# Keeping the issue order of all engines through the last gate units, and five smaller edits

## The chip, the cores and the metric

One core of a Trainium2 chip runs the whole program. The metric is the device time of one execution in microseconds, of which the median of several runs is taken. All arithmetic is float32; TensorE works on pairs of rounded parts (a high part and the low rest, both of type fp32r), three products for one.

## The reference

Three layers follow one another over 4 sequences of 768 tokens. The first is a delta-rule attention with a state of 48 x 48 per head, the second a gated layer that mixes tokens with a 768 x 768 matrix, the third a channel mix with a shift by one token.

```python
for t in range(S):                                     # attention, 4 x 8 heads
    y[t] = q[t] @ state
    state += beta[t] * outer(k_n[t], v[t] - k_n[t] @ state)
h = gelu(x @ w_in); u, v = split(h)                    # gated layer, tanh form of gelu
v_n = (v - mean(v)) / sqrt(var(v) + 1e-6) * g_ln
x = x + (u * (w_sg @ v_n + b_sg)) @ w_out
xk, xr = mix(mu_k, x, x_prev), mix(mu_r, x, x_prev)    # channel mix
out = sigmoid(xr @ w_r) * (relu(xk @ w_k) ** 2 @ w_v)
```

## The kernel before

**Stages.** The attention runs in chunks of 64 tokens, two chunks to a group, six groups (`g`). `run` (L829) issues one stage of each of two streams of chunks, then counts the step `point[0]` up by two in `tick`, and then fills PE's time with `fill` (L680) from the list of gate units. A gate unit is a block of `x @ w_in`: a `v` unit (L611) gives 128 tokens of one sequence, 9 matmuls of 512 columns and then a gelu on ACT (L625); a `u` unit (L662) gives two sequences, 18 matmuls of 256 columns, a gelu (L672) into `ug`, and a store to `u_d`. The attention's result of a group is stored to `xT` (`store_x`, L560); some steps later, by `LAGX` or for the last group `LAGE`, `x_split` (L581) rounds it into `xh` and `xl`, and two steps on the group's units are in the list.

**Rows' scaling.** Each `v` goes through `ln_steps` (L631): bn_stats and bn_aggr on DVE, then for two sequences at once a negated mean and a power of -0.5 on GpSimd (L645 to L648, the exponent is the tile `nhalf`), then `apply` (L651) on ACT (L652) `yield`ed some steps later. The result goes to `vn_d` in DRAM, or, for sequence 0 of the last two groups, straight into a ring block by `to_ring` (L844).

**Weights.** `narrow` (L147) turns a piece of a weight, which comes as 64-bit words, into a high and a low part: load on SP, conversion L157 on ACT, L162, L164, L166, L168 on DVE, an integer add L170 on GpSimd, then `split` (L110) with L113 for the high part on ACT and L116 for the low part on GpSimd. `resident` uses it for `w_in`, `scratch` for the other weights (8 pieces of `w_out` and 12 of `w_k` from the pool `stg`; `w_r` and `w_v` from another pool), which go back to DRAM. A part of the pieces of `scratch` is issued during the attention, the rest by `side` (L968), which `mix` and `project` call.

**Between attention and mixing.** After the attention's scope the kernel opens 8 PSUM banks (`ps`) and the pools `wq2` and `vr` on the memory that the attention's pools `ap1` and `ap2` leave. It loads `b_sb` and the first three blocks of `ws1` (the second half of `w_sg`; `fetch_ws1`, L935, through `staged`, L233), begins the first mixing with 60 matmuls on 4 banks (`begin`, L924), and then loops (L947) until the last gate units are through: `background`, `fill(5)`, and one `split_ws1` (L938) a turn, which rounds a block on ACT and DVE and loads the block three further on. Then `wo` is reloaded on GpSimd's queue, and the mixing runs over 4 sequences x 2 halves of the tokens: `mix` (L994) with 18 matmuls, `w` on DVE (L1004, L1006), `gh` on ACT and `gl` on DVE, and `project` (L1011). From then on comes the channel mix.

**What sets the order.** A planner orders each engine's instructions by modelled times and priorities in program order; a load or an operation further down may go ahead of one that it takes to be not ready. In a `manual_schedule` scope the engines named issue their own instructions of that scope in program order; instructions from outside the scope may still be placed between. SP, which issues most transfers, is in no scope. Before, PE, ACT, DVE and GpSimd are in one during the attention (L244), and PE alone (L892) from there to the end.

Of the kernel before, what the change touches and what calls it, by code (L numbers as in the profile page):

```python
# [7 lines left out]
F32 = mybir.dt.float32  # L8
# [8 lines left out]
B, H, S, D = 4, 8, 768, 48  # L17
DM = 384
FF = 1024
HF = 512  # L20
P = 128
# [25 lines left out]
NT_ = (3, 3, 3)  # L47
LNW = 1
LAGX = 6
LAGE = (4, 1)  # L50
LASTP = 134
FROM = 124
LAGU = 2
# [13 lines left out]
def vw(t, off, dims):  # L67

    a = t[:]
    return bass.AP(a.tensor, a.offset + off, [list(a.ap[0])] + [list(d) for d in dims])  # L70
# [9 lines left out]
def fused_kernel(  # L80
# [17 lines left out]
    nc = tc.nc  # L98
    V, A, G, T = nc.vector, nc.scalar, nc.gpsimd, nc.tensor

    cp = ctx.enter_context(tc.tile_pool(name="cp", bufs=1))
    dp = ctx.enter_context(tc.tile_pool(name="dp", bufs=1, space=bass.MemoryType.DRAM))
    stg = ctx.enter_context(tc.tile_pool(name="stg", bufs=2))
# [6 lines left out]
    def split(eng_hi, eng_lo, src, hi, lo):  # L110

        if eng_hi is A:
            A.activation(hi, src, AF.Copy)  # L113
        else:
            eng_hi.tensor_scalar(hi, src, 1.0, None, op0=ALU.mult)
        eng_lo.tensor_tensor(lo, src, hi.bitcast(F32), op=ALU.subtract)  # L116
# [30 lines left out]
    def narrow(dram, i, j, hi, lo, cw=CW, pool=stg, lag=JLAG, parts=None):  # L147

        w = CW if pool is stg else cw
        raw = pool.tile([P, 2 * w], U32, name="raw", bufs=NRAW if pool is stg else 2)
        nc.sync.dma_start(out=raw[:, :2 * cw], in_=dram[i * P:(i + 1) * P, j:j + cw].bitcast(U32))
        w_lo = vw(raw, 0, [(2, cw)])
        w_hi = vw(raw, 1, [(2, cw)])
        yield 0
        yield 0, lambda: A.activation(w_lo.bitcast(I32), w_lo, AF.Copy, scale=2.0 ** -29)  # L157
        a = pool.tile([P, w], U32, name="na", bufs=NNA if pool is stg else 2)[:, :cw]
        af = a.bitcast(F32)
        t1 = cw / 1920 + 0.16  # L160
        t2 = cw / 960 + 0.16
        V.tensor_scalar(a, w_hi, 0x7FFFFFFF, None, op0=ALU.bitwise_and)  # L162
        yield t1
        V.tensor_scalar(af, af, E_LO_F, E_HI_F, op0=ALU.max, op1=ALU.min)  # L164
        yield t1
        V.tensor_scalar(a, a, 3, 0x3FFFFFFF, op0=ALU.logical_shift_left, op1=ALU.bitwise_and)  # L166
        yield t1
        V.scalar_tensor_tensor(a, w_hi, 0xC0000000, a, op0=ALU.bitwise_and, op1=ALU.bitwise_or)  # L168
        yield t2
        G.tensor_tensor(a.bitcast(I32), a.bitcast(I32), w_lo.bitcast(I32), op=ALU.add)  # L170
        if hi is None:
            hi, lo = (raw[:, e * cw:e * cw + cw].bitcast(F32R) for e in range(2))
            parts.append(raw[:, :2 * cw].bitcast(F32).rearrange("p (x n) -> p x n", x=2))
        yield lag, lambda: split(A, G, af, hi, lo)

    def resident(dram, pool, name, nblk, n, j0=0, j1=None):


        j1 = j1 or n
        hi = pool.tile([P, nblk, j1 - j0], F32R, name=name + "_hi", bufs=1)  # L180
        lo = pool.tile([P, nblk, j1 - j0], F32R, name=name + "_lo", bufs=1)
        return hi, lo, [lambda i=i, j=j: narrow(dram, i, j, hi[:, i, j - j0:j - j0 + CW],
                                                lo[:, i, j - j0:j - j0 + CW], lag=0)
                        for i in range(nblk) for j in range(j0, j1, CW)]
# [16 lines left out]
    def reload(dh, dl, pool, name, nblk, n, tag):  # L201
        parts = []
        for d, x in ((dh, "_hi"), (dl, "_lo")):
            t = pool.tile([P, nblk, n], F32R, name=name + x, tag=tag + x)
            G.dma_start(out=t, in_=d.rearrange("c p n -> p c n"))
            parts.append(t)
        return parts
# [20 lines left out]
    def turn(tiles, shape, dtype=F32):  # L228
        tiles.append(tiles.pop(0))
        pool, tag = tiles[-1]  # L230
        return pool.tile(shape, dtype, name=tag, tag=tag, bufs=1)

    def staged(src, n):  # L233
        x = turn(sts, [P, HF])[:, 0:n]
        nc.sync.dma_start(out=x, in_=src)
        return x

    with ExitStack() as at:
        ap1 = at.enter_context(tc.tile_pool(name="ap1", bufs=1, side="right"))
        ap2 = at.enter_context(tc.tile_pool(name="ap2", bufs=2, side="right"))  # L240
        ps1 = at.enter_context(tc.tile_pool(name="ps1", bufs=1, space=PSUM))
        ps2 = at.enter_context(tc.tile_pool(name="ps2", bufs=2, space=PSUM))
        ET = mybir.EngineType
        at.enter_context(tc.manual_schedule(  # L244
            engines={ET.PE, ET.Activation, ET.DVE, ET.Pool}))

        wv_hi, wv_lo, in_jobs = resident(w_in, fp, "wiv", 3, FF, HF, FF)
        wu_hi, wu_lo, j1 = resident(w_in, fp, "wiu", 3, FF, 0, HF)
        in_jobs += j1
# [57 lines left out]
                    if i == 0:  # L307
                        E.memset(SQ[o][0][h][r:r + 64, :, 0:D], 0.0)
        G.memset(xT[:, :, :, 0:1], 0.0)
        nhalf = ap1.tile([P, B], F32, name="nhalf")  # L310
        G.memset(nhalf, -0.5)

        def gram(g, parts=((0, 64),)):
# [224 lines left out]
        def st_y(s, o):  # L538
# [13 lines left out]
            if s % 2:  # L552
                store_x(g, o, ysts[o])
                after(LAGX if g < NG - 1 else LAGE[o], lambda: splits.append((g, o)))
            if o == 1:
# [20 lines left out]
        later, vstat, streams, point = [], {}, [], [0, 0]  # L576

        def after(n, f):
            later.append((point[0] + n, f))
# [51 lines left out]
        def ln_steps(g, b, v):  # L631
            mv, vs = vstat[g]
            n = 2
            st6 = fp.tile([P, 6], F32, name="st6")
            V.bn_stats(out=st6, in_=v)
            yield 0.6
            V.bn_aggr(out=mv[:, b], in_=st6)
            yield 0.1
            if b % n == n - 1:
                b0 = b + 1 - n  # L640
                var = fp.tile([P, n], F32, name=f"var{n}")
                yield 1, None
                rs = fp.tile([P, n], F32, name=f"rs{n}")
                nm = fp.tile([P, n], F32, name=f"nm{n}")
                G.tensor_scalar(var, mv[:, b0:b + 1, 1], EPS, None, op0=ALU.add)  # L645
                G.tensor_scalar(nm, mv[:, b0:b + 1, 0], -1.0, None, op0=ALU.mult)
                G.tensor_tensor(rs, var, nhalf[:, :n], op=ALU.pow)
                G.tensor_tensor(nm, nm, rs, op=ALU.mult)  # L648
                yield 2, None

                def apply(i):  # L651
                    A.activation(vs[b0 + i], vs[b0 + i], AF.Identity, bias=nm[:, i:i + 1],  # L652
                                 scale=rs[:, i:i + 1])
                    if b0 + i == 0 and g >= NG - 2:
                        to_ring(0, g, vs[0])
                    else:
                        after(1, lambda: nc.sync.dma_start(out=vn_d[b0 + i, g], in_=vs[b0 + i]))

                for i in range(n):
                    yield LNW, lambda i=i: apply(i)  # L660
# [19 lines left out]
        def fill(n):  # L680
            n += owed[0]
            while n > 0 and (units or opened[0]):
                if not opened[0]:
                    done = min([i for i, _ in running] + [n_jobs - len(jobs)])
                    ready = [u for u in units if done >= (6, 12)[u[2]]]
                    if ready:
                        units.remove(ready[0])
                        opened[0] = ready[0][1]()
                    else:
                        break  # L690
                w, f = opened[0].pop(0)
                f()
                n -= w
            owed[0] = min(n, 0)
            if n > 0 and point[0] < 144:
                idle[0] += n
                keep_warm(int(idle[0]))
                idle[0] -= int(idle[0])
# [3 lines left out]
        def keep_warm(n):  # L702

            if n > 0:
                o = bank()[:].rearrange("p a b -> p (a b)")
                for _ in range(n):
                    T.matmul(o, lhsT=warm, rhs=vw(warm, 0, [(0, 4), (1, P)]), start=True, stop=True)
# [136 lines left out]
        def to_ring(b, c, vst):  # L844
            t = turn(rb, [P, 2 * HF], F32R)
            vh, vl = ring[b, c] = (t[:, 0:HF], t[:, HF:2 * HF])
            split(A, G if c % 3 and (b or c > 4) else V, vst, vh, vl)

        def fetch_pair(t, i):
            src = w_sg[2 * i * P:2 * (i + 1) * P, 0:DM].rearrange("(c p) t -> p c t", p=P)  # L850
# [37 lines left out]
            fill(1)  # L888


    pe = ctx.enter_context(ExitStack())
    pe.enter_context(tc.manual_schedule(engines={mybir.EngineType.PE}))  # L892
    ps = ctx.enter_context(tc.tile_pool(name="ps", bufs=8, space=PSUM, reuse_waits="tile"))
    wq2 = ctx.enter_context(tc.tile_pool(name="wq2", bufs=1, side="right", reuse_waits="tile"))
    vx = ExitStack()
# [37 lines left out]
    ahead, got = [], []  # L933
# [13 lines left out]
    while later or splits or units or streams or opened[0]:  # L947
        background(2)
        units.sort(key=lambda u: (u[0][0], u[2]))
        fill(5)  # L950
        point[0] += 1
        if ahead:
            ahead.pop(0)()
    for f in ahead:
        f()
    fl.close()
    wo = reload(wo_dh, wo_dl, wq2, "wo", 4, DM, "w2")

    mx = ExitStack()
# [213 lines left out]
```

## Time and profile before

| | us |
|---|---|
| median of 3 runs | 802.19 |
| lowest and highest | 800.7, 803.46 |
| profiled execution, its time | 803.6 |
| its span | 801.9 |
| PE busy | 721.8 (90%) |
| DVE, ACT, GpSimd busy | 524.5, 359.6, 202.7 |

The span is what the profile covers, from the first to the last instruction. L12 is line 12 of the kernel. PE is TensorE's matmuls, PEld its weight loads, POOL is GpSimd, SP the engine that issues transfers, SPq its queue. The granted clock is a share of TensorE's full clock. A wait is idle time of an engine just before an instruction, put down to the work that ended last before it could start.

### The profile page before, as it was taken

What the parts mean: (1) busy time and instruction counts of PE and PEld (TensorE: products, weight loads), DVE (VectorE), ACT (ScalarE), POOL (GpSimd) and SP (SyncE); (2) the same over time, 40 slices, a digit from 0 to 9 for tenths busy, and PEclk for the clock granted to TensorE, in tenths of its full rate; (3) what the DMA queues carried; (4) which work ended last, traced back from release to release, by engine and by line L of the source; (5) the groups of instructions that cost most, each with busy time, mean ns of one, the idle gap of its engine ahead of it and who ended that gap; (6) DMA issues with size and microseconds to landing.
All of it is one profiled execution on the core that took longest, in us unless ns stands there. A gap on an engine that the chain in (4) does not pass through costs nothing.

```text
span 801.9 us, 23562 instructions
## 1 busy us (share of the span) xinstructions
PE 721.8 (90%) x10126; PEld 655.9 (82%) x10126; DVE 524.5 (65%) x1090; ACT 359.6 (45%) x732; POOL 202.7 (25%) x247
## 2 busy tenths in 40 slices
PE   3478998898989988879869999999999999999998
PEld 3335677777877877769769898899999999999998
DVE  6989679699697896643447684658755555554441
ACT  2225455555655656652523223216644544543330
POOL 3254333344432434442414254211000000000000
PEclk9979999999999989998989989999999999999999
DMA  8323354364463636635596546146200000000000
GB/s 236 81 67 89 95 128 111 105 167 150 114 170 113 170 100 171 187 106 165 173 297 197 180 143 228 62 156 161 67 20 30 11 21 31 11 20 30 11 21 29
DMA packets 82152, 88.66 MB, mean 111 GB/s; under 512 B 24704, under 2 KB 65024, under 8 KB 82048
## 3 DMA queue, kind: packets, MB, share of 16 engines
q1 hardware_dynamic: 76816, 77.92, 32.4%
q0 software_dynamic: 4800, 9.04, 4.1%
q8 instruction: 79, 1.29, 0.7%
q10 hardware_dynamic: 432, 0.20, 0.1%
q14 instruction: 25, 0.20, 0.1%
HBM read 56.60 MB, written 25.82 MB: 103 GB/s over the span
## 4 chain that ended last, share of the span: by engine, by line
PE 52%; DVE 19%; DMA 10%; issue 4%; ACT 4%; POOL 3%; SPq 1%; ACTq 0%; DVEq 0%; POOLq 0%
PE ms L144 33%; PE ms L919 4%; DVE sg L348 3%; PE ms L668 3%; PE rk L456 2%; PE ms L616 2%; DMA raw<-in_w_v_dram 2%; POOL na L170 2%; DMA st<-in_w_sg_dram 2%; PE ms L544 1%; PE sps L530 1%; DVE r L448 1%; PE rk L510 1%; DMA raw<-in_w_r_dram 1%; DVE sg L386 1%
## 5 line engine op out<-in xcount | busy, mean ns | idle before, releaser
L144 PE MATMUL ms<-wvh,sh 128*128 128x384 f32 x192 | 64.9, 338 | 0.0
L144 PE MATMUL ms<-wvl,sh 128*128 128x384 f32 x192 | 64.9, 338 | 0.0
L144 PE MATMUL ms<-wvh,sl 128*128 128x384 f32 x192 | 64.8, 338 | 0.0
L144 PE MATMUL ms<-xm_hi,sw0h 128*128 128x384 f32 x192 | 64.1, 334 | 0.0
L144 PE MATMUL ms<-xm_lo,sw0h 128*128 128x384 f32 x192 | 64.1, 334 | 0.0
L144 PE MATMUL ms<-xm_hi,sw0l 128*128 128x384 f32 x192 | 64.1, 334 | 0.0
L170 POOL TENSOR_TENSOR na<-na,raw 128x256 int32<-128x256 int32 (+2 forms) x43 | 37.1, 863 | 106.7 <-DVE na L168 86.8
L919 PE MATMUL ms<-ws1h,g 128*128 128x384 f32 x192 | 51.1, 340 | 5.8 <-ACT ws1h L113 5.8
L116 DVE TENSOR_TENSOR sl<-sg,sh 128x384 fp32r<-128x384 f32 x64 | 35.6, 557 | 30.3 <-ACT sh L113 30.2
L919 PE MATMUL ms<-sw0h,g 128*128 128x384 f32 x192 | 50.6, 337 | 1.3 <-POOL g L116 1.3
L113 ACT ACTIVATE sh<-sg 128x384 fp32r<-128x384 f32 x64 | 33.5, 524 | 36.3 <-DVE sg L1093 36.3
L448 DVE TENSOR_TENSOR r<-vk,rk 128x384 f32<-128x384 f32 x40 | 21.9, 548 | 40.3 <-PE rk L510 20.7
L1109 DVE TENSOR_TENSOR sg<-sg,ms 128x384 f32<-128x384 f32 x24 | 13.3, 554 | 47.8 <-PE ms L144 47.8
L1093 DVE TENSOR_TENSOR sg<-sg 128x384 f32<-128x384 f32 x64 | 35.3, 552 | 11.4 <-ACT sg L1092 11.3
L348 DVE TENSOR_TENSOR sg<-sg,Yt 128x512 f32<-128x512 f32 (+10 forms) x78 | 41.1, 526 | 2.1
L668 PE MATMUL ms<-xh,wiu_hi 128*128 128x256 f32 x144 | 39.3, 301 | 2.9 <-ACT v L625 2.9
L1092 ACT ACTIVATE sg<-ms 128x384 f32<-128x384 f32 x64 | 30.8, 482 | 24.5 <-PE ms L144 24.5
L919 PEld LDWEIGHTS ms<-ws1h,g 128*128 128x128 f32 x192 | 35.7, 192 | 6.1 <-ACT ws1h L113 6.1
L668 PE MATMUL ms<-xl,wiu_hi 128*128 128x256 f32 x144 | 39.9, 305 | 0.0
L144 PE MATMUL ms<-gh,wo_hi 128*128 128x384 f32 x96 | 34.6, 360 | 4.8 <-ACT gh L113 4.8
L162 DVE TENSOR_SCALAR na<-raw 128x256 uint32<-128x256 uint32 (+2 forms) x43 | 17.2, 403 | 32.1 <-DMA raw<-in_w_v_dram 8.3
L668 PE MATMUL ms<-xh,wiu_lo 128*128 128x256 f32 x144 | 37.9, 291 | 0.0
(222 smaller groups left out, 2237.0 us busy)
## 6 DMA issues: line engine op xcount, KB each, us to landing
u_d<-ug SPq DMA_DIRECT2D x24, 256.0 KB, 2.7
u<-u_d SPq DMA_DIRECT2D x16, 384.0 KB, 4.4
vn_d<-v SPq DMA_DIRECT2D x22, 256.0 KB, 3.0
vk<-in_vk_dram SPq DMA_DIRECT2D x24, 192.0 KB, 3.5
vk<-in_vk_dram SPq DMA_DIRECT2D x12, 384.0 KB, 4.5
out_dram<-sg SPq DMA_DIRECT2D x24, 192.0 KB, 1.9
SQ<-in_q_d_dram SPq DMA_DIRECT2D x36, 96.0 KB, 3.2
xT<-yst SPq DMA_DIRECT2D x23, 144.0 KB, 3.2
```

The costliest lines, as they stand in the source:

```text
L113: A.activation(hi, src, AF.Copy)
L116: eng_lo.tensor_tensor(lo, src, hi.bitcast(F32), op=ALU.subtract)
L144: T.matmul(pt, lhsT=a, rhs=b, start=(i == 0), stop=(i == n - 1))
L162: V.tensor_scalar(a, w_hi, 0x7FFFFFFF, None, op0=ALU.bitwise_and)
L170: G.tensor_tensor(a.bitcast(I32), a.bitcast(I32), w_lo.bitcast(I32), op=ALU.add)
L348: V.tensor_tensor(tv, vw(a_t, a_off, a_dims), vw(b_t, b_off, b_dims), op=ALU.mult)
L448: V.tensor_tensor(t, vt[s][:, 8 * o:8 * o + 8, :], RQs[o], op=ALU.add)
L456: T.matmul(RQs[o][b0:b0 + 32, p, 0:D], lhsT=DT[b0:b0 + 32, u0 + p, :], rhs=t[b0:b0 + 32, p, :], start=True, stop=True, skip_group_check=True)
L668: T.matmul(vstat["u"][:, 2 * P * d:2 * P * d + 2 * P], lhsT=w[:, c, ds_], rhs=a[:, c].rearrange("p b t -> p (b t)"), start=first, stop=last)
L919: T.matmul(pt[:, :DM], lhsT=v[:, ds_], rhs=w, start=(c == 0 and i == 0), stop=(c == 5 and i == 2))
L1092: A.activation(r, pt[:, :DM], AF.Relu)
L1093: V.tensor_tensor(r, r, r, op=ALU.mult)
```

## The change

- The scope that keeps order for PE, ACT, DVE and GpSimd is opened before the attention and closed behind the loop of the last gate units, after which PE alone goes on.
- `nhalf` moves from `ap1` to the pool `cp`, which lives to the end.
- The high parts of the pieces of `w_out` and `w_k` (those of `scratch` from `stg`) are taken by GpSimd instead of ACT.
- `apply` of the scaling comes one step later (`yield 3`).
- The ring blocks of sequence 0 all have their low part on DVE (before, block 5 had it on GpSimd).
- Loads of 384 columns by `staged` (those of `ws1`) are issued by ACT instead of SP.
- In the loop, `fill(9)` instead of `fill(5)`, and `split_ws1` from the second turn on, at its end as before. `LAGE` for the second half of the last group is 3 instead of 1.

```diff
-LAGE = (4, 1)
+LAGE = (4, 3)
@@ narrow
-        yield lag, lambda: split(A, G, af, hi, lo)
+        yield lag, lambda: split(A if parts is None or pool is not stg else G, G, af, hi, lo)
@@ staged
-        nc.sync.dma_start(out=x, in_=src)
+        (nc.scalar if n < HF else nc.sync).dma_start(out=x, in_=src)
@@ ahead of the attention's scope
+    man = ctx.enter_context(ExitStack())
+    ET = mybir.EngineType
+    man.enter_context(tc.manual_schedule(engines={ET.PE, ET.Activation, ET.DVE, ET.Pool}))
@@ in it
-        ET = mybir.EngineType
-        at.enter_context(tc.manual_schedule(
-            engines={ET.PE, ET.Activation, ET.DVE, ET.Pool}))
-        nhalf = ap1.tile([P, B], F32, name="nhalf")
+        nhalf = cp.tile([P, B], F32, name="nhalf")
@@ ln_steps
-                yield 2, None
+                yield 3, None
@@ to_ring
-            split(A, G if c % 3 and (b or c > 4) else V, vst, vh, vl)
+            split(A, G if c % 3 and b else V, vst, vh, vl)
@@ behind the attention
-    pe = ctx.enter_context(ExitStack())
-    pe.enter_context(tc.manual_schedule(engines={mybir.EngineType.PE}))
@@ the loop of the last units
-        fill(5)
+        fill(9)
         point[0] += 1
-        if ahead:
+        if ahead and point[0] > 149:
             ahead.pop(0)()
     for f in ahead:
         f()
     fl.close()
+    man.close()
+    pe = ctx.enter_context(ExitStack())
+    pe.enter_context(tc.manual_schedule(engines={ET.PE}))
```

## Rows read from the trace of the kernel before

**Rows 1.** Busy time by stage: stretch, length, each engine, clock, DMA, GB/s.

```profile
0.00:365.00 365.00, 305.29 (x7786) 246.03 (x7787) 279.66 (x612) 189.78 (x379) 141.82 (x182) 0.96 0.47 131
365.00:417.00 52.00, 42.25 (x240) 39.69 (x240) 20.87 (x46) 20.19 (x38) 16.01 (x23) 0.92 0.69 216
417.00:530.00 113.00, 106.03 (x569) 102.28 (x568) 72.77 (x131) 30.89 (x59) 40.56 (x36) 0.95 0.51 170
530.00:802.00 272.00, 268.25 (x1537) 267.92 (x1535) 151.24 (x303) 118.71 (x256) 4.33 (x6) 1.00 0.13 38
```

**Rows 2.** What PE waited for from 330 us: total us, times, longest.

```profile
PE ms L919 <- ACT ws1h L113: 5.8, 1, 5.8
PE ms L144 <- ACT gh L113: 4.8, 4, 2.0
PE ms L544 <- ACT ug L672: 3.3, 1, 3.3
PE ms L668 <- ACT v L625: 2.9, 2, 2.6
...
PE ms L919 <- POOL g L116: 1.3, 1, 1.3
```

**Rows 3.** Timeline of ACT around 358 us: start, us, engine, line, operation [idle before].

```profile
357.99 0.81 ACT L652 ACTIVATE v<-v,nm,rs 128x512 f32<-128x512 f32 x1 [2.40 <-POOL nm L648]
358.81 0.98 ACT L521 ACTIVATE SQ<-rk 64x384 f32<-64x384 f32 x2
359.81 0.60 ACT L672 ACTIVATE ug<-ms 128x512 f32<-128x512 f32 x1
```

**Rows 4.** Busy time around PE's waits, columns as in group 1.

```profile
361.00:366.00 5.00, 5.00 (x45) 4.88 (x42) 0.00 (x0) 0.74 (x2) 0.00 (x0) 0.50 0.61 165
...
376.00:389.00 13.00, 12.71 (x74) 11.10 (x72) 5.20 (x14) 3.51 (x9) 5.82 (x10) 1.00 0.30 103
389.00:396.00 7.00, 4.64 (x38) 4.61 (x38) 2.19 (x5) 4.67 (x9) 3.18 (x8) 1.00 0.48 135
...
407.50:411.00 3.50, 3.50 (x11) 3.19 (x12) 1.32 (x3) 1.28 (x3) 0.00 (x0) 0.56 0.86 282
```

**Rows 5.** Timeline of ACT, 365 to 425 us.

```profile
381.79 0.44 ACT L157 ACTIVATE raw<-raw 128x256 int32<-128x256 uint32 x1 [3.36 <-DMA raw<-in_w_k_dram]
...
390.01 0.81 ACT L652 ACTIVATE v<-v,nm,rs 128x512 f32<-128x512 f32 x1 [2.40 <-POOL nm L648]
```

**Rows 6.** Timeline of SP's queue, 330 to 425 us.

```profile
392.03 0.33 SPq L657 DMA_DIRECT2D vn_d<-v  x1
...
392.89 0.94 SPq L235 DMA_DIRECT2D st<-in_w_sg_dram  x2
...
399.17 1.46 SPq L235 DMA_DIRECT2D st<-in_w_sg_dram  x2
```

**Rows 7.** DMA issues by line: KB each, median us to landing.

```profile
st<-in_w_sg_dram SPq DMA_DIRECT2D x4, 192.0 KB, 6.3
```

**Rows 8.** Timeline of ACT, 400 to 409 us.

```profile
406.93 0.94 ACT L113 ACTIVATE ws1h<-st 128x384 fp32r<-128x384 f32 x2 [1.59 <-DMA st<-in_w_sg_dram]
```

**Rows 9.** Timeline of POOL, 393.5 to 398 us.

```profile
395.23 1.00 POOL L205 DMA_DIRECT2D wo_hi<-wo_d  x1
396.27 1.27 POOL L116 TENSOR_TENSOR g<-v,g 128x512 fp32r<-128x512 f32 x1
```

**Rows 10.** Timeline of DVE, 372 to 377 us.

```profile
372.98 0.29 DVE L162 TENSOR_SCALAR na<-raw 128x256 uint32<-128x256 uint32 x1 [1.20 <-DMA raw<-in_w_k_dram]
373.30 0.77 DVE L164 TENSOR_SCALAR na<-na 128x256 f32<-128x256 f32 x1
```

**Rows 11.** Timeline of POOL, 365 to 425 us.

```profile
373.18 0.74 POOL L116 TENSOR_TENSOR raw<-na,raw 128x256 fp32r<-128x256 f32 x1 [0.53 <-ACT raw L113]
```

**Rows 12.** Instructions of POOL by form: line, names, shapes, count, busy us, mean ns.

```profile
L116 POOL TENSOR_TENSOR raw<-na,raw 128x256 fp32r<-128x256 f32 x12 | 10.0, 837 | 9.8 <-ACT raw L113 9.3 <-DVE na L166 0.5
```

**Rows 13.** Timeline of DVE, 365 to 425 us.

```profile
413.85 1.03 DVE L1006 TENSOR_TENSOR w<-w,u 128x384 f32<-128x384 f32 x2 [2.46 <-DMA u<-u_d]
```

## The prediction

> **What bounds the kernel now.** I read the busy time by stage first [rows 1]. The reader is to see three things in it. From 530 us on the matrix engine (PE) is busy for 268.25 of 272 us: nothing can be won there, and all that comes earlier before it arrives at the end as it is. From 417 to 530 us it is busy for 106.03 of 113. The hole is the stretch from 365 to 417 us, 42.25 of 52, in which the last gate units run and the mixing of the tokens begins. Then the list of what PE waited for from 330 us on [rows 2]: one wait each of 5.8 us for a rounded block of `w_sg` (`ws1h`), 3.3 for a `ug`, 1.3 for a ring block `g`, 2.9 (two, the longer 2.6) for a `v`, and four for `gh`, 4.8 together. Then the timelines around these waits, on the engine named in them. Last, the granted clock around them [rows 4]: it is 0.50 from 361 to 366 us and 0.56 from 407.5 to 411 us, after the waits of 3.3 and 5.8 us, while after the wait of 2.6 us it is 1.00. So two of the waits also cost time at the lower of the clock's two levels (1.2 instead of 2.4 GHz).
>
> **What stands behind each wait.** ACT does its work in its queue's order. At 357.99 us it runs a scaling of rows (L652) that waited for GpSimd's `nm`, and only behind it the two copies L521 at 358.81 and the `ug` of L672 at 359.81 for which PE waits [rows 3]. By the code this scaling belongs to step 148, behind the scope in which orders are kept, and L521 to step 144: the planner put it in front. At 381.79 us the conversion L157 of a `w_k` piece, which the code issues in `side`, far behind the loop of the last units, has waited 3.36 us for its load; a unit's `v` stands behind it. At 390.01 us a scaling has waited 2.40 us for GpSimd again, with the next `v` behind it [rows 5]. The loads of `ws1` that the code issues ahead of everything in the tail come out of SP only at 392.89, behind a store of `v` at 392.03; the last two follow at 399.17 [rows 6] and are used at 406.93 [rows 8], 7.8 us later. GpSimd issues a load of `wo` (1.00 us) at 395.23, ahead of the ring block's low part at 396.27 [rows 9]. So it is order, and loads issued late, not work.
>
> **The change part by part.** The sum is made against the profiled execution, 803.6 us (span 801.9); the median of the runs is 802.19, that is 1.4 lower, and I carry the difference over unchanged.
>
> A. The kept order puts the two L521 and `ug` ahead of the scaling, and the scaling one step later keeps ACT off GpSimd's chain. What is left of the 3.3 us is `ug` itself, 0.60 [rows 3], and about 0.3 for two hand-overs between engines (0.15 us from its end to PE's start, 360.41 to 360.56, once each way): 0.9. Gain 2.4, bounds 0 and 3.3.
>
> B. With a wait of 0.9 the clock should stay up, as it did after 2.6. At 0.50 the 5.0 us hold 2.5 us of work [rows 4]. Gain 2.5, bounds 0 and 2.5.
>
> C. The wait of 2.6: the `v` activations stand in order behind their matmuls instead of behind a scaling and a conversion, and the first scaling comes one step later than the power. `begin` holds four of the pool's eight PSUM banks, so four are free, and a unit takes about 2.1 us (12.71 us of PE for six units from 376 to 389 us [rows 4]), so ACT may be some 8 us late before PE stands. Gain 2.6, bounds 0 and 2.6.
>
> D. The ring block: its low part goes to DVE, and GpSimd's load of `wo` is out of its way, but its scaling now stands on ACT behind the last `ws1` rounding and the last-but-one `ug`. I count the 1.3 us as kept: 0, bounds -1.3 and +1.3.
>
> E. The six `ws1` loads are issued by ACT in program order, the first three at step 148 (about 366 us, some 26 us sooner than 392.89), the others three units' time ahead of need. Their landing has a median of 6.3 us [rows 7]; three units are 6.4. They get a place to land because `nhalf` no longer holds the recurrence's pool until the last power. What each issue costs ACT is 0.4 to 1.0 us by SP's rows of the same loads (0.94 and 1.46 for two) [rows 6], and each of the last three waits for DVE's low part of the block three before; the activations of `v` and `ug` queue behind that, and the free banks cover it. Gain 5.8, bounds 2 and 5.8.
>
> F. The slow stretch behind that wait: 3.5 us at 0.56, so 1.5 us [rows 4]. Gain 1.5, bounds 0 and 1.5.
>
> G. Twenty high parts go from ACT to GpSimd. No row shows this operation there. GpSimd's low part of the same size takes 0.84 [rows 12], which I take as its price; the lower end is nothing, since ACT no longer waits for GpSimd in the middle of each piece. 15 of the 20 pieces lie before 365 us, where GpSimd is busy for 142 of 365 us [rows 1]; beside work, so 0 there. The other five of `w_k` can still be put between the units, with L157 waiting on ACT (3.36 us [rows 5]) and L162 on DVE: I give back 1.0, bounds 0 and 3.4.
>
> H. If these five are pushed back into the mixing instead, they queue ahead of `w` and `gh` there. Eleven pieces run there now and PE waits 4.8 us for `gh` [rows 2], 0.44 each; five more are 2.2, none is 0. I take 1.2.
>
> Late next would be `u`: DVE waited 2.46 us for it until 413.85 [rows 13], with PE still mixing. Its loads follow the last `u_d` store, which moves forward with the last unit; covered, at 0. `LAGE` 4 and 3 only moves a split behind the first unit, with PE's 60 matmuls of `begin` before it: 0.
>
> Sum: 2.4 + 2.5 + 2.6 + 0 + 5.8 + 1.5 = 14.8 won, 1.0 + 1.2 given back: 12.6. From 803.6 that is 791.0, and from the median 789.6.
>
> **Two rules weighed.** Beside a GpSimd operation of 0.74 us from 373.18 [rows 11], DVE's L164 of 256 columns takes 0.77, and the like L162 just before, alone, 0.29 [rows 10]. The Trainium skill (SBUF — State Buffer, "SBUF: two separate sides") has the reason: the two engines share a port pair which the first holds for its whole instruction. By the rule each moved high part may hold up DVE; by the row that is 0.48 us. It is the slower rival below. On E the Trainium skill speaks against the new queue (DMA: Bandwidth & Descriptors, "Issuing engines are not separate DMA queues"): another issuing engine only saves issue time. By that alone E would be worth nothing and the sum 5.3; the row that decides is the issue at 392.89 behind SP's 392.03, and I count the earlier issue, not the queue.
>
> **The rivals.** *Half the tail stays* (20%): the planner still moves the pieces of `w_k` and SP's stores where it wants, ACT is late by its own waits, and the last three `ws1` blocks each land 7.8 us after issue, as today, against 6.4 of cover. Lost against the forecast: C 2.6, E three times 1.4, together 6.8; 802.19 - 5.8 = 796.4. For it: a non-kept instruction was put in front of kept ones at 357.99. *More is won* (10%): with the loads spread out, the waits for `gh` in the mixing (4.8 [rows 2]) and half of the clock lost there (0.05 of 113 us [rows 1], so 2.8) go too; 7.6 us together: 802.19 - 12.6 - 7.6 = 782.0. *Slower* (7%): GpSimd's added 0.84 and DVE's added 0.48 fall into the recurrence's chain, through the masks (GpSimd) and `r` (DVE) that PE waits for. On the path in all 15 pieces that is 19.8 us: 802.19 - 12.6 + 19.8 = 809.4; it decides from 0.84 us a piece. Against it: GpSimd idles more than half of that stage [rows 1]. *The order is kept, but nothing comes of it* (3%): the loads still wait for the pool's place; about 802.
>
> **How the numbers follow.** The forecast has 60%. The range goes from just short of the better case, 782.5, to the half-won case with its own bound, 798. Under 799.8 lies faster by over 0.3% (2.4 us, about what a measurement of this kernel can tell from no change): 60 + 20 + 10, less 2 for the tail of the half-won case, 0.88. Same 0.05, slower 0.07.
>
> **What would show it.** A: L652 behind the second `ug` on ACT and PE's wait at about 358 us under 1 us. B: granted clock near 1.0 for the five us after. C and E: no PE wait for `v` or `ws1h` over 1 us, and the `ws1` loads issued by ACT near 366 us. D: one wait of about 1 us for `g`. G, H: where the last five `w_k` pieces run, and PE's waits for `gh` against 4.8. From 0 to 340 us the two traces should agree within 1 us, and the stretch after the mixing should be 272 us again. Wrong would be the forecast if the recurrence gets longer, if ACT stands at a `ws1` issue while PE has run out of banks, or if the mixing grows by more than 4 us.

## The result and the profile after

The change made the kernel slower. The median of 20 runs is 810.27 us (803.13 to 816.6) against 802.15 for 20 runs of the kernel before beside them: ratio 1.0088, 95% interval 1.0063 to 1.0112. The forecast was 789.6, in a range up to 798.0. The profiled execution took 807.92 us (span 806.1), 4.3 more than that of before.

Three marks cut both traces into the same parts: the last `yst` copy on ACT (L549 before, L548 after), which ends the recurrence; DVE's first sum of a mixed block into `xT` (L1019), which ends the tail of gate units; and its last.

| us | before | after | difference |
|---|---|---|---|
| last `yst` copy | 362.58 | 367.95 | +5.4 |
| tail, up to the first sum | 58.5 | 61.4 | +2.9 |
| mixing, first to last sum | 138.1 | 134.9 | -3.2 |

Behind the mixing the two agree within 1 us. So the recurrence, whose end was to win the 4.9 us of A and B, lost 5.4, and the tail, which was to win the 9.9 of C, E and F, lost 2.9. (Single executions differ by some us, so verdicts go by the ratios.)

Busy time by stage of the kernel after, columns as in [rows 1]:

```profile
0.00:365.00 365.00, 302.31 (x7737) 243.04 (x7738) 282.13 (x612) 183.78 (x361) 151.22 (x193) 0.93 0.46 129
365.00:417.00 52.00, 41.29 (x245) 37.27 (x245) 18.17 (x40) 18.66 (x34) 19.83 (x31) 0.85 0.70 202
417.00:530.00 113.00, 105.67 (x585) 102.98 (x584) 76.09 (x134) 31.32 (x61) 40.63 (x37) 0.98 0.52 175
530.00:806.00 276.00, 272.18 (x1564) 271.86 (x1562) 152.57 (x305) 118.71 (x256) 4.35 (x6) 1.00 0.14 41
```

The granted clock of the first 365 us fell from 0.96 to 0.93, that of the hole behind it from 0.92 to 0.85, and the hole is as wide as it was: 41.29 of 52 us.

What PE waited for from 330 us on in the kernel after, to be held against [rows 2]:

```profile
PE ms L615 <- ACT xh L113: 6.7, 1, 6.7
PE ms L144 <- ACT gh L113: 4.1, 3, 2.4
PE rk L455 <- DVE r L447: 3.3, 2, 1.7
PE ms L615 <- DVE xl L116: 3.1, 1, 3.1
```

The waits for `ws1h` (5.8), `ug` (3.3) and `v` (2.6) are gone, as forecast. Two stand in their place, 6.7 for `xh` and 3.1 for `xl`; the 3.3 for `r` fell in the recurrence.

**The recurrence.** Until 185 us the `yst` copies of the two traces agree within 1 us; at 205 us the kernel after is 3.5 late, at 243 us 5.5. ACT's timeline shows what happens first, before and then after:

```profile
193.16 0.81 ACT L652 ACTIVATE v<-v,nm,rs 128x512 f32<-128x512 f32 x1
193.89 0.34 ACT L113 ACTIVATE raw<-na 128x192 fp32r<-128x192 f32 x1
194.25 0.61 ACT L335 ACTIVATE sg<-ms 128x256 f32<-128x256 f32 x1
194.66 0.41 ACT L335 ACTIVATE sw0h<-ms 128x256 f32<-128x256 f32 x1
```

```profile
193.16 1.52 ACT L651 ACTIVATE v<-v,nm,rs 128x512 f32<-128x512 f32 x2
194.70 0.61 ACT L334 ACTIVATE sg<-ms 128x256 f32<-128x256 f32 x1
195.10 0.42 ACT L334 ACTIVATE sw0h<-ms 128x256 f32<-128x256 f32 x1
```

Before, one scaling stands ahead of the Gram matrices' copies; after, with `yield 3`, two. The copies start 0.45 us later, and PE, which waits for the second (before, then after):

```profile
195.13 0.50 PE L616 MATMUL ms<-wiv_hi,xh 128*128 128x512 f32 x1 [1.36 <-ACT sw0h L335]
```

```profile
195.57 0.50 PE L615 MATMUL ms<-wiv_hi,xh 128*128 128x512 f32 x1 [1.81 <-ACT sw0h L334]
```

Busy time in stretches behind that wait, the mean granted clock in the third number from the right, before (where the next five microseconds show 1.00 too) and after:

```profile
195.00:200.00 5.00, 4.87 (x137) 4.00 (x137) 4.90 (x5) 2.79 (x7) 2.65 (x2) 1.00 0.34 117
```

```profile
195.00:200.00 5.00, 4.43 (x99) 3.81 (x103) 4.90 (x5) 2.46 (x6) 3.10 (x3) 0.67 0.40 145
200.00:205.00 5.00, 5.00 (x90) 3.86 (x81) 0.20 (x2) 1.46 (x4) 0.00 (x0) 0.65 0.16 43
```

Half a microsecond more of waiting is followed by ten microseconds at two thirds of the clock, which cost 5 x 0.33 + 5 x 0.35 = 3.4 us: the whole lag at 205 us. That the longer wait brought the lower clock is inferred from this order and from the runs below; no run changed the clock alone.

The wait stands at three groups of this trace (near 143, 196 and 253 us), and the clock fell behind the second alone. Over the traces of the six kernels with `yield 3` that are read here, the change and five of those below, these waits take 1.8 to 2.1 us, and the mean granted clock of the ten microseconds behind is 0.66 at 13 of the 18 and 1.00 at the other 5. In the thirteen with `yield 2` or 4 they take 1.1 to 1.4 us, and it is 1.00 at all 39. So single traces spread: the last `yst` copy comes between 366.96 and 374.13 us in the first set and between 356.79 and 366.10 in the second.

**The tail.** The chain of work that ended last, in order of time, kernel after (start, us, what):

```profile
370.75 8.15 DMA raw<-in_w_k_dram
...
379.98 0.44 DVE na L168
...
380.55 0.75 POOL na L170
...
381.39 0.87 POOL raw L115
...
382.33 0.75 POOL raw L116
383.10 0.52 SPq L195
...
383.71 4.77 DMA raw<-in_w_k_dram
```

This is one `w_k` piece of `side`: load, steps on DVE, sum, high part and low part on GpSimd, store, and in SP's queue behind the store the load of the next. ACT's timeline in that stretch:

```profile
385.16 0.44 ACT L157 ACTIVATE raw<-raw 128x256 int32<-128x256 uint32 x1 [5.37 <-DMA raw<-in_w_k_dram]
388.50 0.43 ACT L157 ACTIVATE raw<-raw 128x256 int32<-128x256 uint32 x1 [2.90 <-DMA raw<-in_w_k_dram]
390.46 0.44 ACT L157 ACTIVATE raw<-raw 128x256 int32<-128x256 uint32 x1 [1.53 <-DMA raw<-in_w_k_dram]
390.80 0.57 ACT L624 ACTIVATE v<-ms 128x512 f32<-128x512 f32 x1
...
391.98 0.83 ACT L113 ACTIVATE xh<-xT 128x768 fp32r<-128x768 f32 x1
397.08 0.43 ACT L157 ACTIVATE raw<-raw 128x256 int32<-128x256 uint32 x1 [4.26 <-DMA raw<-in_w_k_dram]
```

Four conversions of pieces hold ACT for 5.37 + 2.90 + 1.53 + 4.26 = 14.1 us, with `v` and the split `xh` that `LAGE` put off queued behind. PE pays there, and again with the clock:

```profile
392.87 1.65 PE L615 MATMUL ms<-wiv_hi,xh 128*128 128x512 f32 x3 [6.69 <-ACT xh L113]
...
398.94 1.65 PE L615 MATMUL ms<-wiv_hi,xl 128*128 128x512 f32 x3 [3.14 <-DVE xl L116]
```

Three such matmuls take 1.65 us here; at 379.73 us, ahead of the wait, the same three took 0.87.

### The profile page after: what moved, and what is told of

The parts are those of the page before. It is cut to its first block, busy times and chain, and to the rows that moved or that the text cites. A ratio compares the mean times of both kernels' runs of the same rounds, so it can differ in the third digit from the quotient of the medians.

```text
span 806.1 us, 23585 instructions
## 1 busy us (share of the span) xinstructions
PE 721.4 (89%) x10126; PEld 655.1 (81%) x10126; DVE 529.0 (66%) x1091; ACT 352.5 (44%) x712; POOL 216.0 (27%) x266
## 4 chain that ended last, share of the span: by engine, by line
PE 57%; DVE 17%; DMA 8%; issue 4%; ACT 3%; POOL 3%; SPq 1%; DVEq 0%; POOLq 0%; ACTq 0%
PE ms L144 33%; PE ms L667 4%; PE ms L916 4%; PE ms L615 4%; DVE sg L347 3%; PE rk L455 3%; DMA raw<-in_w_v_dram 2%; DMA raw<-in_w_k_dram 2%; PE ms L543 2%; PE rk L509 2%; PE sps L529 2%; POOL na L170 1%; PE rk L479 1%; PE ms L325 1%; DVE Yt L385 1%
## 5 line engine op out<-in xcount | busy, mean ns | idle before, releaser
L615 PE MATMUL ms<-wiv_hi,xh 128*128 128x512 f32 x72 | 31.8, 462 | 14.9 <-ACT xh L113 6.7
L1093 DVE TENSOR_TENSOR sg<-sg 128x384 f32<-128x384 f32 x64 | 35.3, 552 | 11.5 <-ACT sg L1092 11.4
L495 POOL TENSOR_SCALAR_AFFINE_SELECT SQ<-SQ 64x512 f32<-64x512 f32 x36 | 28.3, 785 | 44.3 <-ACT SQ L494 43.1
L113 ACT ACTIVATE gh<-w 128x384 fp32r<-128x384 f32 x32 | 16.5, 522 | 52.5 <-DVE w L1006 52.5
```

The lines of the kernel that those rows point to most:

```text
L495: G.affine_select(out=pt, in_=pt, pattern=[[0, 8], [1, C]], compare_op=ALU.is_gt, fill=0.0, base=0, channel_multiplier=-1)
L615: T.matmul(vstat[g, b], lhsT=a[:, c], rhs=w[:, c], start=first, stop=last)
L1093: V.tensor_tensor(r, r, r, op=ALU.mult)
```

## The experiments

Eighteen kernels. Ratios are to the kernel before, run beside each on the same chip; the change itself stands at 1.0088. "Kept order alone" is the kernel before with the scope of kept orders through the last units, `nhalf` in `cp`, and nothing else; no run takes these two apart.

**Does the delayed split hold the tail?**

```diff
-LAGE = (4, 3)
+LAGE = (4, 1)
```

> The changed kernel with LAGE = (4, 1) again. Theory of the tail: with the kept order the split of the last group's second half stands on ACT behind the first v activation, and that one behind four conversions (L157) of w_k pieces that wait 14.1 us together for their loads; PE then waits 6.7 us for xh and 3.1 for xl and runs some 5 us at the lower clock. With the split ahead of the first v activation both waits go; what comes next is a late v, of 0 to 4 us: 801 to 805 us against 810.3. Theory of the recurrence (the loss lies ahead of 365 us): nothing before the tail moves, so at most 2 us are won: 808 to 811.

1.0112 (1.0077 to 1.0147), 809.9 us. The waits for `xh` and `xl` went, and PE waited 8.0 us for `v` and 3.4 for `g` instead. `LAGE` decides only which instruction stands behind the conversions.

**Are the pieces the cause in the tail?** The seven pieces of `side`, two of which the planner had put ahead of the tail, get their tiles from a pool that is free only behind it:

```diff
+    late = [stg]
...
-            yield from narrow(dram, i, j, None, None, cw, pool, parts=parts)
+            yield from narrow(dram, i, j, None, None, cw, late[0] if pool is stg else pool, ...)
...
+    late[0] = st
```

> The changed kernel with the seven w_k pieces that side issues taken from the pool st, which exists only behind the tail, so that none can be placed between the last units. Theory of the tail: ACT's 14 us of waits for raw loads go, the split comes in time, PE's waits of 6.7 and 3.1 us go: 798 to 803 us, with 1 to 3 us given back where the seven pieces now stand in the mixing. Theory of the recurrence: the first 330 us stay as in the changed kernel, 806 to 810.

1.0084 (1.0055 to 1.0113), 808.5 us. The tail is 51.0 us instead of 61.4, and PE's waits for `xh` and `xl` are gone: the cause of the longer tail is shown. But mixing takes 147.9 instead of 134.9, with waits for `gh` and `gl` of 13.6 us from 330 us on (5.7 in the changed kernel). The work was moved, and its price with it.

**Is the scaling the cause in the recurrence?** Back to two steps:

```diff
-                yield 3, None
+                yield 2, None
```

> The changed kernel with the scaling one step earlier again (yield 2). Theory of the recurrence: the later step put two scalings instead of one ahead of the copies of L334 in each of the middle groups, PE waits 1.81 instead of 1.36 us there and the granted clock falls behind it in some of the groups; with yield 2 the stretch up to the last yst is again some 5 us shorter: 804 to 806. Theory of the tail: the tail keeps its waits for xh and xl, so 808 to 811.

1.0140 (1.0104 to 1.0176), 811.1 us: no gain. The last `yst` copy came at 363.98, 4 us earlier, but the tail took 62.9, with PE waiting 6.3 us for `xl` and 3.7 for `xh`.

**Do the high parts on GpSimd cost anything?**

```diff
-        yield lag, lambda: split(A if parts is None or pool is not stg else G, G, af, hi, lo)
+        yield lag, lambda: split(A, G, af, hi, lo)
```

> The changed kernel with the high parts of the w_out and w_k pieces on ACT again. If GpSimd's added high parts (0.70 to 0.85 us each in the trace) and what they hold up on DVE cost time in the recurrence, 4 to 6 us come back: 804 to 806. If not, 809 to 812, as ACT gets 20 roundings of 0.34 to 0.42 us back and waits for GpSimd in the tail again.

1.0123 (1.0095 to 1.0152), 810.5 us: seemingly nothing. I called them neutral after this run, and that was a mistake, as the last runs show.

**One part of the change alone.** First the scaling, on the kernel before:

```diff
-                yield 2, None
+                yield 3, None
```

> The kernel before with nothing but the later scaling (yield 3). If the later scaling is what makes the recurrence longer (it puts two scalings ahead of the copies of L334, PE's wait there grows from 1.36 to 1.81 us and the granted clock falls behind it), the last yst comes 3 to 6 us later and the time is 804 to 807 us against 801 to 802. If the longer recurrence of the changed kernel comes from the clock's chance or from another edit, 800 to 803.

1.0195 (1.0174 to 1.0216), 819.3 us, 12 more than the upper end of what was expected. It is the worst of all the kernels: last `yst` copy at 373.69, the copies waited for 2.1 us.

Then the kept order alone:

```diff
+    man = ctx.enter_context(ExitStack())
+    man.enter_context(tc.manual_schedule(engines={ET.PE, ET.Activation, ET.DVE, ET.Pool}))
     with ExitStack() as at:
...
-        nhalf = ap1.tile([P, B], F32, name="nhalf")
+        nhalf = cp.tile([P, B], F32, name="nhalf")
...
     fl.close()
+    man.close()
```

> The kernel before with the kept order through the last units and nhalf in cp, and no other edit (fill(5), LAGE (4, 1), yield 2, loads by SP, high parts by ACT as before). If the order as such is the loss (the activations stand behind the conversions of w_k pieces placed between them, PE waits for v), 805 to 810 us. If the order wins what the prediction said (the waits of 3.3 and 5.8 us go) and the loss lies in the other edits, 793 to 799.

0.9911 (0.9895 to 0.9928), 796.6 us: 7 us faster. PE's waits from 360 to 420 us in this kernel:

```profile
PE ms L144 <- ACT gh L113: 5.2, 2, 4.6
PE ms L667 <- ACT v L624: 3.2, 2, 2.7
```

The waits for `ws1h` and `ug` are gone (0.19 us are left of the latter), that for `v` stays, and the longest for `gh`, 2.0 before, is 4.6. It stands behind DVE, which waits for the `u` that is loaded from `u_d`:

```profile
406.61 1.03 DVE L1006 TENSOR_TENSOR w<-w,u 128x384 f32<-128x384 f32 x2 [13.18 <-DMA u<-u_d]
```

So of the 8.3 us between this trace and that of before, 5.8 lie ahead of the last `yst` copy (356.79), with the clock at 1.00 behind it, and the tail wins 1.5 (57.0 instead of 58.5). The loads of `ws1` now leave SP early, the first two as SP's queue shows here and the third at 369.56, without ACT issuing any:

```profile
365.98 1.16 SPq L235 DMA_DIRECT2D st<-in_w_sg_dram  x2
```

**Scaling and pieces together.** The changed kernel with both `yield 2` and the late pieces:

> The changed kernel with the last seven w_k pieces behind the tail and yield 2. If the two losses are separate, the recurrence gets its 4 us back and the tail its 10, of which the mixing gives back about as much: 803 to 806 us, and the last yst at 361 to 365 us. If the later scaling is not what lengthens the recurrence, 808 to 810 as with the late pieces alone.

0.9974 (0.9950 to 0.9999), 801.1 us; last `yst` copy at 360.59, tail 49.8, mixing 146.3.

**Pieces sooner, not later.** Two instead of seven pieces are left for the tail, the others run in the recurrence, where ACT was busy for 184 and DVE for 282 of 365 us:

```diff
-EVERY = 12
-RUN = (3, 1, 2)
+EVERY = 6
+RUN = (3, 2, 2)
```

> The changed kernel with two pieces at a time in the attention (EVERY = 6, RUN = (3, 2, 2)), so that two instead of seven w_k pieces are left for side. Theory of the tail: ACT's waits for raw loads between the last units fall from 14 us to at most 5, PE's waits for xh and xl shrink to 0 to 4 us, and the mixing has no piece more than now: 6 to 10 us won there. The five more pieces cost DVE about 1.5 us each in the recurrence, where it is busy for 83%: 0 to 6 us lost. 799 to 808 us; the first product of the projection within 55 us of the last yst, against 61 now.

0.9897 (0.9870 to 0.9924), 795.8 us: tail 53.8, mixing 129.8, though `yield 3` still ends the recurrence at 372.71. With `yield 2` as well:

> The changed kernel with the scaling put back one group (yield 2) and only two w_k pieces left for the tail instead of seven. Theory (two losses that add: the scaling's place in ACT's queue, worth about 10 us before the last yst copy, and the pieces that are placed among the kept instructions, worth about 14 us when moved ahead): last yst copy near 361 us instead of 372.7 (the earlier pieces with yield 3), and a median of 783 to 790 us. Rival (the tail falls back when the recurrence ends earlier, as it did with yield 2 alone: 62.9 us of tail): last yst copy near 361 us, but a tail over 60 us or mixing over 135 us, and a median of 795 us or more.

0.9775 (0.9747 to 0.9804), 785.6 us. Last `yst` copy at 360.59, tail 53.4, mixing 131.2, all as the theory had it. And the same two numbers on top of the kept order alone:

> The kernel before with the kept order through the last gate units alone, and two instead of seven w_k pieces left for the tail. Theory (the kept order is the gain and the pieces placed in it the remaining loss): last yst copy near 360 us, tail 52 to 55 us, median 785 to 792 us, faster than the kept order alone (796.6). Rival (the pieces done earlier cost the recurrence or mixing what they free in the tail): median within 3 us of 796.6.

0.9716 (0.9688 to 0.9743), 780.0 us, better than forecast and the fastest of all, 22 us under the kernel before. Its waits of PE from 330 us on:

```profile
PE ms L144 <- ACT gh L113: 3.6, 2, 2.2
PE ms L144 <- DVE gl L116: 1.2, 2, 0.6
```

**Place in the queue, or lateness?** The kernel before with `yield 4` puts a single scaling ahead of the copies again, though it runs later still:

> The kernel before with yield 4 in place of yield 2, nothing else. By the order of issue, one scaling (L652) stands ahead of each pair of gram's copies (L335) again, where yield 3 puts two there. Theory (what costs is the place in ACT's queue, two scalings of 0.81 us ahead of the copies that TensorE waits for): waits of L616 for L335 back at about 1.4 us, last yst copy within 4 us of the kernel before (359 to 366), median 797 to 808 us. Rival (what costs is that the rows are scaled late, whoever stands ahead of whom): last yst copy at 374 us or later and a median of 819 us or more, at least that of yield 3.

1.0064 (1.0040 to 1.0087), 807.4 us; the lateness rival, 819 or more, falls. ACT around the same group with `yield 3`, then with `yield 4`:

```profile
198.96 0.81 ACT L652 ACTIVATE v<-v,nm,rs 128x512 f32<-128x512 f32 x1
199.68 0.35 ACT L113 ACTIVATE raw<-na 128x192 fp32r<-128x192 f32 x1
199.93 0.80 ACT L652 ACTIVATE v<-v,nm,rs 128x512 f32<-128x512 f32 x1
200.75 0.61 ACT L335 ACTIVATE sg<-ms 128x256 f32<-128x256 f32 x1
```

```profile
193.35 0.37 ACT L113 ACTIVATE raw<-na 128x192 fp32r<-128x192 f32 x1
193.62 0.80 ACT L652 ACTIVATE v<-v,nm,rs 128x512 f32<-128x512 f32 x1
194.44 0.62 ACT L335 ACTIVATE sg<-ms 128x256 f32<-128x256 f32 x1
```

And the clock behind it, `yield 3` and `yield 4`:

```profile
205.00:210.00 5.00, 5.00 (x78) 3.79 (x78) 1.02 (x3) 1.54 (x4) 0.00 (x0) 0.50 0.10 32
```

```profile
205.00:210.00 5.00, 5.00 (x133) 4.60 (x133) 2.46 (x6) 2.25 (x6) 0.13 (x1) 1.00 0.35 76
```

PE's wait is 2.07 us in the first and 1.37 in the second; the clock falls behind two of the three such waits in the first trace and behind none in the second. The last `yst` copy is at 366.1, by 0.1 beyond what the theory allowed: of the 16 us that `yield 3` cost, about 11 (1.31% of 802) are the place in the queue, and the other 5 are not explained.

**What else lies between 811 and 796.6?** `yield 2` with the whole rest of the change is 14 us slower than the kept order alone. First `LAGE` (4, 1) on top of `yield 2`:

> The changed kernel with yield 2 and LAGE (4, 1), both as before. Theory (LAGE alone was neutral only because the wait for v took its place; with the recurrence 10 us shorter the delayed split still holds TensorE by 3.7 and 6.3 us): the xh and xl waits go, tail under 58 us, median 800 to 805 us. Rival (the ACT wait at the pieces' conversions bounds the tail whichever kept instruction is behind it): another wait of 6 us or more for v or g stands in the tail, which stays at 61 us or more, and the median is within 3 us of the 811 us that yield 2 alone gave.

1.0057 (1.0033 to 1.0080), 808.2 us: the rival held, with a wait of 8.0 us for `v` and a tail of 64.7. Then one part at a time on top of the kept order alone (0.9911). The `ws1` splits held back:

```diff
-        fill(5)
+        fill(9)
...
-        if ahead:
+        if ahead and point[0] > 149:
```

> Kept order alone, with the ws1 splits held back past step 149 and nine units per fill instead of five, their loads still by SP. Theory A (the splits held back only move work that is free in the tail): median within 3 us of 796.6. Theory B (held back, they stand behind the conversions of the pieces that wait for their loads, as in the changed kernel, where v waited 8.0 us): tail over 60 us, median 801 to 808 us.

0.9912 (0.9885 to 0.9939), 797.0 us: nothing. The same with the `ws1` loads issued by ACT:

> The same with the ws1 loads issued by ACT. Theory A (three issues before a wait cost ACT 1.3 us where it is idle, as in the changed kernel at 376 us): within 2 us of the run with the loads on SP. Theory B (ACT's queue stands at later issues between gelus): 3 us or more above it, with PE waits for v or ug in the tail.

0.9933 (0.9908 to 0.9958), 798.8 us: no gain from the other engine. The Trainium skill says as much (DMA: Bandwidth & Descriptors, "Issuing engines are not separate DMA queues"). The loads come early by the kept order, with `nhalf` moved. The scaling:

> Kept order alone, with yield 3. Theory (the scaling's place in ACT's queue costs the recurrence whatever the tail does): waits of L615 for L334 at 1.8 us or more, last yst copy at 367 us or later, median 804 to 812 us. Rival (the kept order makes up for it, so the loss of yield 3 alone was that of its tail): last yst copy before 363 us, median within 3 us of 796.6.

1.0028 (0.9994 to 1.0062), so 1.2% on top of the kept order, some 9.5 us, as the theory had it. One of its twelve runs took 797.4 us, the others 806.4 to 810.7, so by the median of all, 809.1, it would be 1.5%; its trace, of the longest, is not read. And the high parts on GpSimd:

> Kept order alone, with the high parts of the w_k pieces on GpSimd as well. Theory A (the high parts lengthen each piece on GpSimd by 0.85 us and hold back the low parts, so the store of a piece and the load of the next): tail over 60 us, against 57.0 with the kept order alone, median 801 to 808 us. Theory B (they are neutral, as the changed kernel with the high parts back on ACT at 810.5 us suggests): median within 3 us of 796.6.

1.0067 (1.0042 to 1.0092), 809.2 us: +1.6%. Last `yst` copy at 361.88, 5.1 later than with the kept order alone, and a tail of 65.7 instead of 57.0. GpSimd just ahead of the tail in this kernel:

```profile
353.72 0.73 POOL L170 TENSOR_TENSOR na<-na,raw 128x256 int32<-128x256 int32 x1
354.54 0.85 POOL L115 TENSOR_SCALAR raw<-na 128x256 fp32r<-128x256 f32 x1
355.48 0.73 POOL L116 TENSOR_TENSOR raw<-na,raw 128x256 fp32r<-128x256 f32 x1
```

Each piece takes 2.3 us of GpSimd instead of 1.5. Three of them end together and late, SP stands at their stores, and the next loads follow far behind in its queue (SP's queue, then ACT):

```profile
353.78 5.87 SPq L195 DMA_DIRECT2D wk_d<-raw  x3
...
375.91 1.57 SPq L153 DMA_DIRECT2D raw<-in_w_k_dram  x3
387.43 6.27 SPq L195 DMA_DIRECT2D wk_d<-raw  x3
```

```profile
383.21 0.44 ACT L157 ACTIVATE raw<-raw 128x256 int32<-128x256 uint32 x1 [8.77 <-DMA raw<-in_w_k_dram]
...
397.40 0.43 ACT L157 ACTIVATE raw<-raw 128x256 int32<-128x256 uint32 x1 [10.24 <-DMA raw<-in_w_k_dram]
```

In the kept order alone, SP had stored two pieces by 351.7 us and issued the next load at 359.58; there the longest of ACT's waits for a piece was 4.5 us. Here PE waits 8.0 us for `v` at 399.57. The last two runs give GpSimd the high parts of one stretch each, by a switch at the `ws1` stage:

```diff
+    hi_on = [G]      # in the other run [A]
...
-        yield lag, lambda: split(A if parts is None or pool is not stg else G, G, af, hi, lo)
+        yield lag, lambda: split(A if parts is None or pool is not stg else hi_on[0], G, af, hi, lo)
...
+    hi_on[0] = A     # in the other run G
```

> Kept order alone, with the high parts on GpSimd only for the pieces that run before the stage of the ws1 blocks (15 operations), those behind on ACT. Theory A (the recurrence loses by GpSimd's added work, as the slower rival of the forecast had it): last yst copy near 362 us, tail at 57 us, median near 802. Theory B (the loss is the tail's alone): last yst copy near 357 us, median within 3 us of 796.6.

> Kept order alone, with the high parts on GpSimd only for the pieces that run with the last gate units and behind (8 operations). Theory A (the tail's loss comes from these: high, low and sum of a piece one behind the other on GpSimd, their stores and the next loads in SP's queue behind them): last yst copy near 357 us, tail at 63 us or more, median near 804. Theory B (the tail's loss comes from the state in which the recurrence leaves the pieces: three at once): tail at 57 to 59 us, median within 3 us of 796.6.

The traces have 13 high parts on GpSimd in the one run and 7 in the other, those of the pieces of `side`, not 15 and 8 as expected. Those of the recurrence alone: 1.0023 (0.9999 to 1.0046), 804.6 us, last `yst` copy at 363.53, tail 58.2. Those of the tail alone: 0.9935 (0.9913 to 0.9957), 797.2 us, tail 58.0. So by the ratios about 9 of the 12.6 us come with the 13 alone and 1.9 with the 7 alone, while the tail's loss of 8.7 stands only in the trace with both. Late loads by themselves don't make it: with the 13 alone three loads leave SP together at 378 us too, and ACT waits 6.75 us for the first, but the next such wait is 1.42 us, where it is 10.24 with both.

**The parts don't add up.** On the kept order, `yield 3` costs 1.2% and the high parts 1.6%, and together with it they cost no more: in the changed kernel, taking the high parts back to ACT makes it no better (1.0123 against 1.0088). Added up, kept order, scaling, high parts and ACT's issues (0.2%) give +2.05%, 16.4 us; 7.1 were measured. From the run with ACT's issues (0.9933) the changed kernel differs by the scaling, the high parts, `LAGE` and one ring block, and these four together cost 1.55%, 12.4 us, about what the high parts cost alone. With `yield 3` an ACT high part of 0.35 us stands between the two scalings (the rows of `yield 3` above), and the copies are waited for 2.1 us with it and 1.8 without. That fits the direction; the rest of the overlap is not explained, and `LAGE` and the ring block have no run of their own on the kept order.

## Why the prediction was wrong

- **The step that failed: `yield 3`.** It was counted as a help in A and C and nowhere as a cost. I looked at what the scaling waits for, not at what is queued behind it: in the recurrence, ACT's copies for which PE waits at once. The text said that until 340 us the traces agree within 1 us; they do until 185. That "the recurrence gets longer" stood among the ways to be wrong, without a price or a place. On the kept order it costs 9.5 us (1.2%): two scalings ahead of the copies, 0.45 to 0.7 us more of PE's waiting in each of three groups, and 3.4 us of clock behind most of them.
- **G, sized at 1.0 us.** The row was there: one wait of 3.36 us at an L157 [rows 5], and five pieces to come. Five such waits are 17 us; 14.1 were measured. I took it that free PSUM banks would cover ACT's lateness, as in C; by the estimate there four banks cover some 8 us, and ACT waited 14.1. The bound of 3.4 was the price of one piece, not of five.
- **G, the high parts in the recurrence at 0.** Their price was right (0.85 us measured, 0.84 taken), but GpSimd idle for more than half of the stage was no cover. On the kept order this part costs 12.6 us, and there the slower rival has its place: PE's waits for `r` from 60 to 440 us are 13.9 us with it (11.4 with the 13 of the recurrence alone) and 9.4 without. The rest no run takes apart; the traces show the chain of a piece (sum, high, low, store, next load) in the tail. Beside `yield 3` taking the part back gains nothing (1.0123 against 1.0088), so that the rival's 809.4 is near the time is in good part luck: with the earlier pieces, where the scaling alone differs, the recurrence ends at 372.71 with `yield 3` and at 360.59 with 2.
- **H, 1.2 us.** Pieces pushed into mixing cost 13.0 us there, all seven of them (the late pieces), 1.9 each where 0.44 was taken; in the changed kernel they were not pushed.
- **A and B, right.** With the kept order alone the wait for `ug` is 0.19 us, the clock stays at 1.00 behind it, and the last `yst` copy comes 5.8 us earlier, where 4.9 were counted; some of that is the spread of single traces.
- **C, E, F: the waits were right, their worth was not.** The kept order alone gained 7 us of the 14.8 counted, and its tail 1.5 of 9.9. The wait of 5.8 us for `ws1h` went, but the late `u`, put at 0 as covered, took its place with 4.6 us of PE's waiting for `gh`, and 2.7 of the wait for `v` stayed. In the changed kernel and with the earlier pieces 1.4 us are left of that wait for `gh`. For E the reason was the order: SP's loads come as early once orders are kept and `nhalf` is moved, and ACT's queue added nothing. The rule that was weighed against E was right about the queue.
- **D, 0.** The waits for ring blocks from 330 us on are 2.3 us in the changed kernel (1.6 for ACT's part, 0.7 for DVE's) instead of 1.3, inside its bounds.
- **`LAGE` at 0.** By itself it is 0 (1.0112 and 1.0088 overlap), as taken, but for another reason: something else stands behind the conversions if the split doesn't.
- **The rival "half the tail stays"** named the true cause in the tail, the planner still moving the pieces, but gave it 6.8 us where ACT waited 14.1.

## What to carry to other kernels

A step that is put off lands at a new place in its engine's queue in every turn of the loop that uses it, not only where it hurt: look up what stands behind that place, and whether the bounding engine waits for it. If an order is kept on some engines while other work is still placed into it by a planner, that work waits for its loads in front of the kept instructions; look whether it can be taken out of the stretch (here to earlier, which added 15.6 us by the ratios to the 7 of the order). A half-idle engine was no cover here for one more link in a chain of load, split and store. And when a wait goes, look up what comes in second behind it.

## What the runs showed of the hardware

- Behind waits of PE of 1.81 and 2.07 us in the recurrence the mean granted clock of five microseconds was 0.65 and 0.50 (0.50 is the lower level, 1.2 instead of 2.4 GHz); behind waits of 1.36 and 1.37 at the same place it stayed at 1.00, and in the tail of before behind one of 2.6 as well [rows 4]. So 0.45 us more of waiting went with 3.4 us of lost clock. It fell behind 13 of 18 waits of 1.8 to 2.1 us there and behind none of 39 of 1.1 to 1.4, so the length of a wait alone doesn't tell which it will be.
- GpSimd takes longer for a high part of one input (0.85 us for 128x256) than for a sum of two inputs of the same size (0.73).
- An operation of DVE on 128x512 that takes 0.68 us elsewhere in that stretch took 1.86 beside GpSimd's split of `xl`, in the kept order with the high parts on GpSimd (POOL, then DVE):

```profile
228.75 1.68 POOL L116 TENSOR_TENSOR xl<-xT,xh 128x768 fp32r<-128x768 f32 x1 [6.35 <-DMA kT<-in_kt_d_dram]
```

```profile
229.11 1.86 DVE L347 TENSOR_TENSOR sg<-sg,Yt 128x512 f32<-128x512 f32 x1
```

The Trainium skill (SBUF — State Buffer, "SBUF: two separate sides") has the two engines shut each other out for whole instructions, and this pair agrees: DVE's ends 0.54 us after GpSimd's, at 230.97 against 230.43, near the 0.68 that it takes alone. No run here tells what this costs in all.
